# Two block products ahead of the attention, the gate in one piece, and w_v and k squared at other offsets

## The chip, the core and the metric

The kernel runs on one core of a Trainium2 chip. A core has TensorE (PE; its weight loads are listed apart as PEld), VectorE (DVE), ScalarE (ACT), GpSimd (POOL) and DMA queues fed from SyncE (SP). The metric is the device time of one execution in microseconds (us), the median of the runs shown.

## The reference

Local attention in chunks feeds a channel mix of the RWKV kind. Cut to what matters:

```python
# q, k, v: [4, 8, 768, 64]; mem_k, mem_v: [4, 8, 8, 64]; chunks of 32, 16 keys left, 8 right, 8 memory keys
for c in range(nc):
    k_full = concat([mem_k, k[:, :, l_start:r_end]]); v_full = concat([mem_v, v[:, :, l_start:r_end]])
    a = softmax(scale * q_c @ k_full.T)
    out[:, :, c_start:c_end] = a @ v_full
x = out as [4, 768, 512]                       # 3072 tokens
x_prev = x shifted by one token
xk = mu_k * x + (1 - mu_k) * x_prev
xr = mu_r * x + (1 - mu_r) * x_prev
k = relu(xk @ w_k)                             # 512 -> 1024
v = (k * k) @ w_v                              # 1024 -> 512
return sigmoid(xr @ w_r) * v                   # gate: 512 -> 512
```

## The kernel before

The 3072 tokens are worked in 12 units u of 256. Tensors are kept in float32; each operand of a large product is split into a high part in fp32r (names with h: `xh`, `wkh`, `kh`) and the rest (`xl`, `wkl`, `kl`), and a product is three products: high by high, high by low, low by high.

A unit's work on TensorE consists of the hidden product `h` (tile `ph`, four pieces, line 594), the gate `g` (`pr`, two halves, line 570), and the value product `v`. In units 0 to 2 `v` is plain (`pv`, line 570). From unit 3 (`FAST`) on, `seven` makes it as a product of 2x2 blocks by Winograd's scheme: seven block products `v{u}.0` to `v{u}.6` (`part`, line 901, tiles `pa`, `pb`, `pc`, `pd`, twelve instructions of 128x256 each) instead of eight. Their stationary operands are blocks of k squared and sums of them (`a11`, `a12`, `a22`, `s1` to `s4`), made by VectorE in place in the two halves of `k2` (line 865) and split into tile `khl` (`operand`, lines 853 and 857). Their moving operands are quarters of `w_v`, or sums of quarters (`wtbig`, `wtx`) made once by `weight_sums`. `add` and `mul` gather the seven results in the output tiles `o` on VectorE (lines 925 and 936).

Among these stands the attention of later units: `s` (scores of unit u+2, line 406), `t` (transposed probabilities, tile `pt`, line 468), copies of `pt` into block-diagonal tiles `aTz` (`bd`, lines 310 and 312), `a` (tile `px`, line 485), and copies of `px` into `xT`. VectorE and ScalarE also do the softmax (`max`, `sub`, `exp`, `sum`, `norm`), the mix (`df`, `mix`), the splits `xh` and `xl`, and the ReLU, square and sigmoid.

Three things set the order. `te_order` writes out the order of the pieces on TensorE and gives each a due time. A planner (`Plan.order`) then places every operation on its engine by costs and due times, chooses between ACT, DVE and POOL where `either` allows it, and hands out buffers in rings. PSUM has 8 banks of 2 KB per partition: tag `s` two, tag `m` four (`ph`, `pr`, `pv`, and some block products), tag `tp` two (`pt`, `px`, and the others). A bank is taken over when its last reader is done. Each engine then runs its instructions in the planned order.

`split_tiles` and the `const.tile` lines place the weights in SBUF in the order in which they are called; `split_x` and `split_k` cut operands out of tiles at an offset of some elements of 4 bytes.

Of the kernel before, what the change touches and what calls it, by code (L numbers as in the profile page):

```python
# [16 lines left out]
P = 128  # L17
# [192 lines left out]
def te_order():  # L210

    nu = B * S // UTOK
    seq = LEAD.split()
    seq = [tuple([x[0]] + [int(n) for n in x[1:].split(".")]) for x in seq]
    for u in range(1, nu):
        a, b = 2 * u + 2, 2 * u + 3
        g = [("g", u + 1, c) for c in range(QPU) if u + 1 < FAST]
        h = [("h", u, f) for f in range(FT // 2)]
        v = [("v", u, n) for n in range(FT // 2)]
        x = [("a", a), ("a", b)]  # L220
        if u >= FAST:
            g = [("g", u, c) for c in range(QPU)]
            v = [("v", u, n) for n in range(7)]
            seq += h + [("t", a), ("t", b), ("s", u + 2), g[0]] + v[:2] + x + g[1:] + v[2:]
            continue
        seq += h + [("t", a), ("t", b), ("s", u + 2)]
        seq += x + g + v[1:] if u == 1 else v[:1] + x + v[1:] + g
    last = {"s": nu, "g": nu, "t": B * NQT, "a": B * NQT}
    seq = [x for x in seq if x[1] < last.get(x[0], nu)]
    due, t = {}, 8.0  # L230
    for x in seq:
        assert x not in due
        due[x] = t
        t += PART if x[0] == "v" and x[1] >= FAST else PE_COST[x[0]]
    return due
# [3 lines left out]
def local_attention__then__channel_mix(  # L239
# [22 lines left out]
    def sb(tag, shape, name, dt=F32):  # L262
        if isinstance(tag, Slot):
            tag = f"{tag.tag}at{tag.place}"
        return work.tile(shape, dt, tag=tag, name=name, bufs=bufs.get(tag, 1))

    def split_x(tag, name, m):
        if m:
            return sb(tag, [P, KT, UTOK], name, F32R)
        x = sb(tag, [P, 128 + KT * UTOK], name, F32R)  # L270
        return x[:, 48 : 48 + KT * UTOK].rearrange("p (k t) -> p k t", k=KT)

    def split_k(tag, name):
        n = 2 * (int(tag[2:])) + "hl".index(tag[1])
        return khl[:, 16 + n * DM : 16 + (n + 1) * DM]

    def ps(tag, name, n=1):
        return psA.tile([P, n * 512], F32, tag=tag, name=name, bufs=bufs[tag])
# [4 lines left out]
    def split_tiles(n, name):  # L283
        return [
            [const.tile([P, 2 * DM], F32R, tag=f"{name}{s}{i}", name=f"{name}{s}{i}") for i in range(n)]
            for s in "hl"
        ]

    wk_hl, wv_hl, wr_hl = split_tiles(KT, "wk"), split_tiles(FT // 2, "wv"), split_tiles(KT // 2, "wr")
    aTz = [  # L290
        const.tile([P, NPAIR * NJ, 2, CHUNK], F32, tag=f"aTz{i}", name=f"aTz{i}")
        for i in range(bufs["aT"])
# [15 lines left out]
    def copy(e, dst, src):  # L308
        if e is nc.scalar:
            e.copy(dst, src)  # L310
        else:
            e.tensor_copy(dst, src)  # L312
# [248 lines left out]
    def channel_mix(u):  # L561
# [115 lines left out]
        for f in range(FT // 2):  # L677
            def f_relu(e, f=f):
                half = k2[f // 2].rearrange("p i t -> p (i t)")
                r = T["kf", u, f] = half[:, f % 2 * 2 * UTOK : (f % 2 + 1) * 2 * UTOK]  # L680
                if e is nc.scalar:
                    e.activation(r, T["ph", u, f], AF.Relu)  # L682
                else:
                    e.tensor_scalar_max(r, T["ph", u, f], 0.0)  # L684

            def f_sq(e, f=f):
                q = T["kf", u, f]
                if e is nc.scalar:
                    e.activation(q, q, AF.Square)  # L689
                else:  # L690
                    e.tensor_mul(q, q, q)  # L691

            def f_hi(e, f=f):
                h = T["kh", u, f] = split_k(f"kh{f}", f"kh{u}_{f}")
                copy(e, h, T["kf", u, f])

            def f_lo(e, f=f):
                l = T["kl", u, f] = split_k(f"kl{f}", f"kl{u}_{f}")
                e.tensor_sub(l, T["kf", u, f], T["kh", u, f].bitcast(F32))

# [12 lines left out]

# [122 lines left out]
    def seven(u, ks, o_g, sgs):  # L836
# [6 lines left out]
        def operand(name, at, pair, deps):  # L843
            src = A[at]
            kh, kl = Slot(f"kh{pair}"), Slot(f"kl{pair}")
            use = kf[2 * at[1] : 2 * at[1] + 2]

            def view(x):
                return x.rearrange("p (i t) -> p i t", t=P)

            def f_hi(e):
                T["ah", u, name] = view(split_k(kh.tag, f"kh{u}_{name}"))
                copy(e, T["ah", u, name], src)

            def f_lo(e):
                T["al", u, name] = view(split_k(kl.tag, f"kl{u}_{name}"))
                e.tensor_sub(T["al", u, name], src, T["ah", u, name].bitcast(F32))  # L857

            hh = op(f"kh{u}.{name}", either(act=(0.6,), dve=(0.36, True)), f_hi, deps, new=[kh], use=use)
            ll = op(f"kl{u}.{name}", either(dve=(0.62, True), pool=(1.3, True)), f_lo, [hh], new=[kl], use=use + [kh])  # L860
            return hh, ll, kh, kl

        def step(name, out, x, y, deps):
            def f():
                nc.vector.tensor_sub(A[out], A[x], A[y]) if name != "s1" else nc.vector.tensor_add(A[out], A[x], A[y])  # L865

            return op(f"{name}{u}", ("dve", 0.62, True), f, deps, use=kf)

        sq = [x for x, _ in ks]
        a11 = operand("a11", (0, 0), 0, sq[:2])  # L870
        a12 = operand("a12", (0, 1), 1, sq[2:])
        a22 = operand("a22", (1, 1), 2, sq[2:])
        s1 = step("s1", (1, 1), (1, 0), (1, 1), sq[:2] + [a22[1]])
        s3 = step("s3", (1, 0), (0, 0), (1, 0), [s1])
        o1 = operand("s1", (1, 1), 3, [s1])
        s2 = step("s2", (0, 0), (1, 1), (0, 0), [s1, s3, a11[1]])
        s4 = step("s4", (0, 1), (0, 1), (0, 0), [s2, a12[1]])

        def bank(key, tag):
            T[key, u] = ps(tag, f"{key}{u}")  # L880
# [58 lines left out]
                f"{name}u{u}", ("dve", 0.37, True), f, [dep, o_g[at[0]]], use=[os[at[0]], sgs], due=dep.due + 0.6,  # L939
            )  # L940

        def f_keep(e):
            copy(e, spot((0, 1)), T["pa", u][:, :HN])

        os = [Slot("o") for _ in range(QPU)]
        pa, pb, pc, pd = Slot("tp"), Slot("m"), Slot("m"), Slot("tp")
        p1 = part(0, "a11", a11, (0, 0), "pa", 0, pa, [], "tp")
        k1 = op(
            f"keep{u}", either(act=(0.4,), dve=(0.36,)), f_keep, [p1], new=opens(0), use=[pa, os[0]],
            due=p1.due + PART + 0.6,  # L950
        )
        p2 = part(1, "a12", a12, (1, 0), "pa", 1, pa, [])
        c11 = add("c11", (0, 0), (0, 1), "pa", 1, pa, [p2, k1])
        o3 = operand("s3", (1, 0), 0, [s3, p1])
        o2 = operand("s2", (0, 0), 1, [s2, p2])
        p7 = part(2, "s3", o3, 3, "pb", 0, pb, [], "m")
        o4 = operand("s4", (0, 1), 0, [s4, p7])
        p6 = part(3, "s2", o2, 2, "pb", 1, pb, [])
        u2 = add("u2", (1, 0), (0, 1), "pb", 1, pb, [p6, k1])
        p5 = part(4, "s1", o1, 1, "pc", 0, pc, [], "m")  # L960
        u4 = add("u4", (0, 1), (1, 0), "pc", 0, pc, [p5, u2, c11])
        c22 = add("c22", (1, 1), (0, 1), "pb", 0, pb, [u4, p7])
        u3 = add("u3", (1, 0), (1, 0), "pb", 0, pb, [u4, p7])
        p3 = part(5, "s4", o4, (1, 1), "pd", 0, pd, [], "tp")
        c12 = add("c12", (0, 1), (0, 1), "pd", 0, pd, [p3, c22])
        p4 = part(6, "a22", a22, 4, "pc", 1, pc, [])
        c21 = add("c21", (1, 0), (1, 0), "pc", 1, pc, [p4, u3])
        muls = [mul("m11", (0, 0), c11), mul("m22", (1, 1), c22), mul("m12", (0, 1), c12), mul("m21", (1, 0), c21)]
        for c, deps in ((0, [muls[0], muls[2]]), (1, [muls[1], muls[3]])):
            def f_st(c=c):  # L970
# [77 lines left out]
```

## Time and profile before

| | before |
|---|---|
| median of 3 runs | 418.65 us (415.96 to 419.8) |
| the profiled execution, its own time | 418.19 us |
| its span, first to last instruction | 416.3 us |
| mean granted TensorE clock | 0.995 |
| busy: PE, PEld, DVE, ACT, POOL | 399.3, 361.8, 321.8, 207.7, 50.9 us |
| a unit of the second half (units 4 to 9), ph to ph | 31.96 us |

The page gives busy times as shares of the span; the chain of work is followed back from the last instruction; the waits say which engine stood for whom. A row of the time line begins with the start and the duration in us; in the chain likewise. Times between two starts on the same engine tell more of TensorE than durations do, since its products overlap.

### The profile page before, as it was taken

Reading aid. Unit: us, or ns where it says so; the run is one execution under the profiler, and the core shown is the slowest. Engines: PE = TensorE matmul, PEld = TensorE weight load, DVE = VectorE, ACT = ScalarE, POOL = GpSimd, SP = SyncE. Lnnn points to the kernel's source line nnn. Section 1 sums busy time; section 2 is a strip of 40 time slices with the busy share of each in tenths; the row PEclk is TensorE's granted clock in tenths of the full one; section 3 lists DMA queues with packets and bytes.
Section 4 is the critical chain, followed back from the end, with each engine's and each line's share of the span. In section 5 each row is a group of like instructions: output and inputs, shape, how many; then the busy total and the mean of one; then the engine's idle time right before and its main releaser. Section 6 shows DMA issues by size and latency. Waiting matters only on the chain.

```text
span 416.3 us, 10814 instructions
## 1 busy us (share of the span) xinstructions
PE 399.3 (96%) x4787; PEld 361.8 (87%) x4787; DVE 321.8 (77%) x546; ACT 207.7 (50%) x309; POOL 50.9 (12%) x40
## 2 busy tenths in 40 slices
PE   7788999999999999999999999999999999999995
PEld 3446989888988989989989989989989988999995
DVE  3998979997779899489489489479579569669264
ACT  2385792842452763563563554464455455452440
POOL 2202000000000022022022031030130230210000
PEclk9998999999999999999999999999999999999999
DMA  8997955210043070160151152142143103100101
GB/s 328 382 415 249 393 167 177 76 50 27 25 169 138 2 237 18 52 224 31 52 205 52 52 189 66 52 163 93 52 154 101 52 3 102 51 2 2 52 0 50
DMA packets 12910, 48.99 MB, mean 118 GB/s; under 512 B 1472, under 2 KB 1600, under 8 KB 12352
## 3 DMA queue, kind: packets, MB, share of 16 engines
q1 hardware_dynamic: 12864, 48.31, 32.1%
q8 instruction: 37, 0.61, 0.6%
q14 instruction: 9, 0.07, 0.1%
HBM read 42.01 MB, written 6.29 MB: 116 GB/s over the span
## 4 chain that ended last, share of the span: by engine, by line
PE 87%; DVE 6%; DMA 4%; issue 1%; SPq 0%; ACT 0%; DVEq 0%
PE ph L594 32%; PE pr L570 16%; PE pv L570 8%; PE pc L901 6%; PE pb L901 6%; PE pa L901 5%; DMA qk<-in_qk_dram 4%; PE s L406 4%; PE px L485 4%; PE pd L901 3%; PE pt L468 2%; DVE k L865 1%; DVE o L925 1%; DVE khl L312 1%; DVE o L312 1%
## 5 line engine op out<-in xcount | busy, mean ns | idle before, releaser
L594 PE MATMUL ph<-xl,wkh 128*128 128x256 f32 x384 | 106.7, 278 | 0.0
L594 PE MATMUL ph<-xh,wkh 128*128 128x256 f32 x384 | 106.6, 278 | 0.0
L594 PE MATMUL ph<-xh,wkl 128*128 128x256 f32 x384 | 106.4, 277 | 0.0
L594 PEld LDWEIGHTS ph<-xh,wkh 128*128 128x128 f32 x384 | 72.4, 188 | 0.1
L594 PEld LDWEIGHTS ph<-xl,wkh 128*128 128x128 f32 x384 | 72.1, 188 | 0.3 <-DVE xl L553 0.2
L594 PEld LDWEIGHTS ph<-xh,wkl 128*128 128x128 f32 x384 | 72.1, 188 | 0.0
L682 ACT ACTIVATE k<-ph 128x512 f32<-128x512 f32 x45 | 26.9, 597 | 69.2 <-PE ph L594 69.1
L857 DVE TENSOR_TENSOR khl<-k,khl 128x512 fp32r<-128x512 f32 x49 | 32.9, 684 | 22.8 <-ACT khl L310 22.6
L310 ACT CAST khl<-k 128x512 fp32r<-128x512 f32 x54 | 33.4, 618 | 16.6 <-DVE k L865 5.8
L570 PE MATMUL pr<-wrh,xh 128*128 128x512 f32 x96 | 39.6, 412 | 0.0
L570 PE MATMUL pr<-wrl,xh 128*128 128x512 f32 x96 | 37.8, 393 | 0.0
L570 PE MATMUL pr<-wrh,xl 128*128 128x512 f32 (+1 forms) x108 | 37.6, 366 | 0.0
L485 PEld LDWEIGHTS px<-aTz,vw 128*64 128x64 f32 x768 | 25.0, 141 | 10.9 <-DVE o L925 5.4
L312 DVE COPY aTz<-pt 64x512 f32<-64x512 f32 x18 | 11.7, 691 | 29.1 <-ACT aTz L310 29.1
L553 POOL TENSOR_TENSOR xl<-df,xh 128x1024 fp32r<-128x1024 f32 x8 | 19.1, 2391 | 118.1 <-ACT xh L310 118.1
L485 PE MATMUL px<-aTz,vw 128*64 128x64 f32 x768 | 27.9, 229 | 5.6 <-DVE o L925 4.5
L641 ACT ACTIVATE sg<-pr 128x512 f32<-128x512 f32 x24 | 14.3, 599 | 36.5 <-PE pr L570 36.5
L570 PE MATMUL pv<-wvh,khl 128*128 128x512 f32 (+1 forms) x97 | 31.0, 395 | 0.0
L691 POOL TENSOR_TENSOR k<-k 128x512 f32<-128x512 f32 x9 | 9.4, 1039 | 175.3 <-ACT k L682 175.3
L689 ACT ACTIVATE k<-k 128x512 f32<-128x512 f32 x38 | 23.9, 632 | 8.1 <-DVE k L684 7.0
L901 PE MATMUL pa<-wvh,khl 128*128 128x256 f32 x144 | 26.9, 281 | 0.0
L441 DVE TENSOR_TENSOR e<-e,sm_sb 128x1024 f32<-128x1024 f32 x12 | 26.3, 2188 | 0.1
(94 smaller groups left out, 805.5 us busy)
## 6 DMA issues: line engine op xcount, KB each, us to landing
qk<-in_qk_dram SPq DMA_DIRECT2D x24, 768.0 KB, 6.2
vw<-in_vw_dram SPq DMA_DIRECT2D x24, 512.0 KB, 4.2
out_dram<-o SPq DMA_DIRECT2D x24, 256.0 KB, 2.0
raw<-in_w_k_dram SPq DMA_DIRECT2D x4, 1024.0 KB, 8.1
raw<-in_w_v_dram SPq DMA_DIRECT2D x4, 1024.0 KB, 6.7
raw<-in_w_r_dram SPq DMA_DIRECT2D x2, 1024.0 KB, 7.6
id_sb<-in_ident_dram SPq DMA_DIRECT2D x1, 64.0 KB, 6.1
mu_sb<-in_mu_dram SPq DMA_DIRECT2D x1, 4.0 KB, 5.8
```

The lines of the kernel that those rows point to most:

```text
L310: e.copy(dst, src)
L312: e.tensor_copy(dst, src)
L406: nc.tensor.matmul(s5[CHUNK * j : CHUNK * (j + 1), h, c, r, :], q4[z, r, j, :], k4[z, r, j, :], start=True, stop=True,)
L441: g.tensor_mul(e, e, T["sum", u].unsqueeze(2).to_broadcast([P, NG, NK]))
L485: nc.tensor.matmul(p3[64 * h : 64 * h + 64, 2 * g : 2 * g + 2, CHUNK * j : CHUNK * j + CHUNK], v[:, g, h, j, :], a[:, h, g, j, :], start=True,
L553: e.tensor_sub(l, T["xf", u, m], T["xh", u, m].bitcast(F32))
L570: nc.tensor.matmul(p[:, a : a + step], x, w[:, a : a + step], start=start, stop=stop and a + step == DM)
L594: nc.tensor.matmul(z, w, x[:, k], start=start, stop=stop)
L682: e.activation(r, T["ph", u, f], AF.Relu)
L689: e.activation(q, q, AF.Square)
L857: e.tensor_sub(T["al", u, name], src, T["ah", u, name].bitcast(F32))
L901: nc.tensor.matmul(p, l[:, i], r[i], start=i + k == 0, stop=i == FT // 2 - 1 and k == 2)
```

## The change

The order on TensorE from unit 3 on, the scheme's order of steps and of block products, the PSUM tags and the places in SBUF change; the number of instructions on TensorE does not. In the diff, `step`, `operand`, `part`, `add` and `mul` are those shown above.

```diff
@@ te_order
-            seq += h + [("t", a), ("t", b), ("s", u + 2), g[0]] + v[:2] + x + g[1:] + v[2:]
+            seq += h + [("t", a), ("t", b)] + v[:2] + x + [("s", u + 2)] + g + v[2:]
@@ split_x, split_k
-        if m:
-            return sb(tag, [P, KT, UTOK], name, F32R)
-        x = sb(tag, [P, 128 + KT * UTOK], name, F32R)
-        return x[:, 48 : 48 + KT * UTOK].rearrange("p (k t) -> p k t", k=KT)
+        x = sb(tag, [P, 64 * m + KT * UTOK], name, F32R)
+        return x[:, 16 * m : 16 * m + KT * UTOK].rearrange("p (k t) -> p k t", k=KT)
-    def split_k(tag, name):
+    def split_k(tag, off=0):
         n = 2 * (int(tag[2:])) + "hl".index(tag[1])
-        return khl[:, 16 + n * DM : 16 + (n + 1) * DM]
+        return khl[:, off + n * DM : off + (n + 1) * DM]
@@ tiles
-    wk_hl, wv_hl, wr_hl = split_tiles(KT, "wk"), split_tiles(FT // 2, "wv"), split_tiles(KT // 2, "wr")
+    wk_hl, wr_hl = split_tiles(KT, "wk"), split_tiles(KT // 2, "wr")
...
     zero_sb = const.tile([P, P], F32R, tag="zero", name="zero_sb")
+    const.tile([P, 48], F32, tag="gap", name="gap")
+    wv_hl = split_tiles(FT // 2, "wv")
@@ seven
-        a12 = operand("a12", (0, 1), 1, sq[2:])
-        a22 = operand("a22", (1, 1), 2, sq[2:])
-        s1 = step("s1", (1, 1), (1, 0), (1, 1), sq[:2] + [a22[1]])
-        s3 = step("s3", (1, 0), (0, 0), (1, 0), [s1])
-        o1 = operand("s1", (1, 1), 3, [s1])
-        s2 = step("s2", (0, 0), (1, 1), (0, 0), [s1, s3, a11[1]])
-        s4 = step("s4", (0, 1), (0, 1), (0, 0), [s2, a12[1]])
+        s3 = step("s3", (0, 0), (0, 0), (1, 0), sq[:2] + [a11[1]])
+        o3 = operand("s3", (0, 0), 1, [s3])
+        a12 = operand("a12", (0, 1), 2, sq[2:])
+        a22 = operand("a22", (1, 1), 3, sq[2:])
+        s1 = step("s1", (1, 0), (1, 0), (1, 1), [s3] + sq[2:])
+        s2 = step("s2", (1, 1), (1, 1), (0, 0), [s1, a22[1]])
+        s4 = step("s4", (0, 1), (0, 1), (1, 1), [s2, a12[1]])
...
-        pa, pb, pc, pd = Slot("tp"), Slot("m"), Slot("m"), Slot("tp")
-        p1 = part(0, "a11", a11, (0, 0), "pa", 0, pa, [], "tp")
-        p2 = part(1, "a12", a12, (1, 0), "pa", 1, pa, [])
-        c11 = add("c11", (0, 0), (0, 1), "pa", 1, pa, [p2, k1])
-        p7 = part(2, "s3", o3, 3, "pb", 0, pb, [], "m")
-        p6 = part(3, "s2", o2, 2, "pb", 1, pb, [])
-        p5 = part(4, "s1", o1, 1, "pc", 0, pc, [], "m")
-        p3 = part(5, "s4", o4, (1, 1), "pd", 0, pd, [], "tp")
-        p4 = part(6, "a22", a22, 4, "pc", 1, pc, [])
+        pa, pb, pc, pd = Slot("m"), Slot("m"), Slot("tp"), Slot("tp")
+        p1 = part(0, "a11", a11, (0, 0), "pa", 0, pa, [], "m")
+        k1 = keep("ka", (0, 1), 0, p1)
+        p7 = part(1, "s3", o3, 3, "pa", 1, pa, [])
+        k7 = keep("kb", (1, 1), 1, p7)
+        p2 = part(2, "a12", a12, (1, 0), "pb", 0, pb, [], "m")
+        c11 = add("c11", (0, 0), (0, 1), "pb", 0, pb, [p2, k1])
+        p6 = part(3, "s2", o2, 2, "pb", 1, pb, [])
+        p5 = part(4, "s1", o1, 1, "pc", 0, pc, [], "tp")
+        u3 = add2("u3", (1, 0), (1, 0), (1, 1), [u4, k7])
+        p3 = part(5, "s4", o4, (1, 1), "pc", 1, pc, [])
+        p4 = part(6, "a22", a22, 4, "pd", 0, pd, [], "tp")
```

The offset `off` is 48 elements for `pv` (line 694) and 0 for the block products. `keep` copies one side of `pa` into `o`, on ScalarE or VectorE; before, side 0 was copied so and side 1 (the sum c11) was added to it by VectorE from the bank. `add2` is `add` with both inputs in `o`.

Three places show how instructions move. The first is TensorE in unit 7, from the transposes of the probabilities (`pt16`, `pt17`) on; a row is line, operation, output and inputs, shape, and a count. Before:

```order
L468 MATMUL pt16_3336<-id_sb_64,e8_3024 128x128 x4
L468 MATMUL pt17_3342<-id_sb_64,e8_3024 128x128 x4
L406 MATMUL s9_3349<-qk18_3021 32x64 x32
L406 MATMUL s9_3349<-qk19_3027 32x64 x32
L570 MATMUL pr_7_0_3417<-wrh0_82,xh7_1_3213 128x512
```

Now block products (`pa7`) stand there:

```order
L468 MATMUL pt16_3344<-id_sb_64,e8_3135 128x128 x4
L468 MATMUL pt17_3350<-id_sb_64,e8_3135 128x128 x4
L901 MATMUL pa7_3357<-wvh0_86,khl_83 128x256
L901 MATMUL pa7_3357<-wvl0_90,khl_83 128x256
L901 MATMUL pa7_3357<-wvh0_86,khl_83 128x256 x2
```

and behind the 24 products of `pa7`:

```order
L901 MATMUL pa7_3357<-wtx42_1152,khl_83 128x256
L485 MATMUL px16_3392<-aTz0_78,vw16_3020 64x2x32 x16
L485 MATMUL px17_3413<-aTz1_79,vw17_3091 64x2x32 x16
L406 MATMUL s9_3437<-qk18_3108 32x64 x32
L406 MATMUL s9_3437<-qk19_3117 32x64 x32
L570 MATMUL pr_7_0_3509<-wrh0_74,xh7_1_3189 128x512
```

So the scores `s9` and the first gate half moved behind `px`, and both gate halves follow each other; before, `pa7` and the two `px` stood between the halves.

The second place is VectorE in the same unit, around the split of the next unit's `xl8_0` and that of the operand `s4` (an `L857` row that reads `k21`, the second half of k squared). Before, from the step `s4` (`L865`) on:

```order
L865 TENSOR_TENSOR k21_89<-k21_89,k20_88 128x4x128
L533 TENSOR_TENSOR df8_3540<-xT8_3515 128x1024
L435 TENSOR_REDUCE sm_sb_90<-e9_3437 128x16
L436 TENSOR_SCALAR sm_sb_90<-sm_sb_90 128x16
L437 RECIPROCAL sm_sb_90<-sm_sb_90 128x16
L543 SCALAR_TENSOR_TENSOR xf8_3571<-df8_3540,mu_sb_65,xT8_3515 128x256 x4
L857 TENSOR_TENSOR khl_91<-k21_89,khl_91 128x512
L925 TENSOR_TENSOR o7_1_3593<-pb7_3545,o7_0_3472 128x256
L543 SCALAR_TENSOR_TENSOR df8_3540<-df8_3540,mu_sb_65,xT8_3515 128x256 x4
L553 TENSOR_TENSOR xl8_0_3624<-xf8_3571,xh8_0_3591 128x1024
L925 TENSOR_TENSOR o7_0_3472<-pc7_3577,o7_1_3593 128x256
```

and now, from the split of the operand `s2` to that of the operand `s4`, the last row:

```order
L857 TENSOR_TENSOR khl_83<-k21_81,khl_83 128x512
L533 TENSOR_TENSOR df8_3507<-xT8_3430 128x1024
L415 MEMSET s9_3437 32x2x4x16
L419 TENSOR_REDUCE sm_sb_82<-s9_3437 128x16
L543 SCALAR_TENSOR_TENSOR xf8_3526<-df8_3507,mu_sb_65,xT8_3430 128x256 x4
L423 TENSOR_TENSOR e9_3549<-s9_3437,sm_sb_82 128x1024
L543 SCALAR_TENSOR_TENSOR df8_3507<-df8_3507,mu_sb_65,xT8_3430 128x256 x4
L553 TENSOR_TENSOR xl8_0_3572<-xf8_3526,xh8_0_3551 128x1024
L925 TENSOR_TENSOR o7_0_3387<-pb7_3557,o7_0_3387 128x256
L312 CAST khl_83<-k21_81 128x512
L936 TENSOR_TENSOR o7_0_3387<-o7_0_3387,sg7_3547 128x256
L857 TENSOR_TENSOR khl_83<-k21_81,khl_83 128x512
```

The softmax's reduction and subtraction (`L419`, `L423`), both mixes (`L543`) and the split `xl8_0` (`L553`) now stand ahead of the first sum out of `pb7` (`L925`, c11) and the split of `s4`; before, `xl8_0` came behind the latter.

The third place is GpSimd. Before, from the square of units 2 and 3 to the two splits of unit 4:

```order
L691 TENSOR_TENSOR k21_89<-k21_89 128x512 x2
L857 TENSOR_TENSOR khl_91<-k21_89,khl_91 128x512 x2
L553 TENSOR_TENSOR xl4_1_2008<-df4_1906,xh4_1_1975 128x1024
L691 TENSOR_TENSOR k21_89<-k21_89 128x512
L857 TENSOR_TENSOR khl_91<-k21_89,khl_91 128x512 x2
```

and so on in every unit up to 10. Now, from the splits at the program's start to its end:

```order
L365 TENSOR_TENSOR wkl1_71<-mag3_190,wkh1_67 128x1024
L553 TENSOR_TENSOR xl0_0_452<-df0_360,xh0_0_450 128x1024
L691 TENSOR_TENSOR k21_81<-k21_81 128x512 x9
L1055 UNCONDITIONAL_BRANCH
L1055 ISA
```

One square (`L691`) a unit stays on GpSimd; `xl` and two splits into `khl` went to VectorE.

More of the change, by code (lines that the diff above doesn't have):

```diff
@@ L693, in f_hi @@
             def f_hi(e, f=f):
-                h = T["kh", u, f] = split_k(f"kh{f}", f"kh{u}_{f}")
+                h = T["kh", u, f] = split_k(f"kh{f}", 48)
                 copy(e, h, T["kf", u, f])
             def f_lo(e, f=f):
-                l = T["kl", u, f] = split_k(f"kl{f}", f"kl{u}_{f}")
+                l = T["kl", u, f] = split_k(f"kl{f}", 48)
                 e.tensor_sub(l, T["kf", u, f], T["kh", u, f].bitcast(F32))
@@ L851, in f_hi @@
             def f_hi(e):
-                T["ah", u, name] = view(split_k(kh.tag, f"kh{u}_{name}"))
+                T["ah", u, name] = view(split_k(kh.tag))
                 copy(e, T["ah", u, name], src)
             def f_lo(e):
-                T["al", u, name] = view(split_k(kl.tag, f"kl{u}_{name}"))
+                T["al", u, name] = view(split_k(kl.tag))
                 e.tensor_sub(T["al", u, name], src, T["ah", u, name].bitcast(F32))
@@ L940, in mul @@
             )
-        def f_keep(e):
-            copy(e, spot((0, 1)), T["pa", u][:, :HN])
-        os = [Slot("o") for _ in range(QPU)]
-        pa, pb, pc, pd = Slot("tp"), Slot("m"), Slot("m"), Slot("tp")
-        p1 = part(0, "a11", a11, (0, 0), "pa", 0, pa, [], "tp")
[L948 to L951, printed above, removed]
-        p2 = part(1, "a12", a12, (1, 0), "pa", 1, pa, [])
@@ L953, in seven, with keep @@
-        c11 = add("c11", (0, 0), (0, 1), "pa", 1, pa, [p2, k1])
-        o3 = operand("s3", (1, 0), 0, [s3, p1])
-        o2 = operand("s2", (0, 0), 1, [s2, p2])
-        p7 = part(2, "s3", o3, 3, "pb", 0, pb, [], "m")
-        o4 = operand("s4", (0, 1), 0, [s4, p7])
+        def keep(name, at, side, dep):
+            return op(
+                f"{name}{u}", either(act=(0.4,), dve=(0.36,)),
+                lambda e: copy(e, spot(at), T["pa", u][:, side * HN : (side + 1) * HN]), [dep],
+                new=opens(at[0]), use=[pa, os[at[0]]], due=dep.due + PART + 0.6,
+            )
@@ new lines, in add2, with f @@
+        def add2(name, to, x, y, deps):
+            def f():
+                nc.vector.tensor_add(spot(to), spot(x), spot(y))
+            return op(
+                f"{name}u{u}", ("dve", 0.37, True), f, deps, use=[os[at[0]] for at in (to, x, y)],
+                due=deps[0].due + 0.6,
+            )
+        os = [Slot("o") for _ in range(QPU)]
+        pa, pb, pc, pd = Slot("m"), Slot("m"), Slot("tp"), Slot("tp")
+        p1 = part(0, "a11", a11, (0, 0), "pa", 0, pa, [], "m")
+        k1 = keep("ka", (0, 1), 0, p1)
@@ L958, in seven @@
+        p7 = part(1, "s3", o3, 3, "pa", 1, pa, [])
+        k7 = keep("kb", (1, 1), 1, p7)
+        o1 = operand("s1", (1, 0), 0, [s1, p1])
+        o2 = operand("s2", (1, 1), 1, [s2, p7])
+        p2 = part(2, "a12", a12, (1, 0), "pb", 0, pb, [], "m")
+        c11 = add("c11", (0, 0), (0, 1), "pb", 0, pb, [p2, k1])
+        o4 = operand("s4", (0, 1), 2, [s4, p2])
         p6 = part(3, "s2", o2, 2, "pb", 1, pb, [])
         u2 = add("u2", (1, 0), (0, 1), "pb", 1, pb, [p6, k1])
-        p5 = part(4, "s1", o1, 1, "pc", 0, pc, [], "m")
+        p5 = part(4, "s1", o1, 1, "pc", 0, pc, [], "tp")
@@ L961, in seven @@
         u4 = add("u4", (0, 1), (1, 0), "pc", 0, pc, [p5, u2, c11])
-        c22 = add("c22", (1, 1), (0, 1), "pb", 0, pb, [u4, p7])
-        u3 = add("u3", (1, 0), (1, 0), "pb", 0, pb, [u4, p7])
-        p3 = part(5, "s4", o4, (1, 1), "pd", 0, pd, [], "tp")
-        c12 = add("c12", (0, 1), (0, 1), "pd", 0, pd, [p3, c22])
-        p4 = part(6, "a22", a22, 4, "pc", 1, pc, [])
-        c21 = add("c21", (1, 0), (1, 0), "pc", 1, pc, [p4, u3])
+        u3 = add2("u3", (1, 0), (1, 0), (1, 1), [u4, k7])
@@ L968, in seven @@
+        c22 = add2("c22", (1, 1), (0, 1), (1, 1), [u4, u3])
+        p3 = part(5, "s4", o4, (1, 1), "pc", 1, pc, [])
+        c12 = add("c12", (0, 1), (0, 1), "pc", 1, pc, [p3, c22])
+        p4 = part(6, "a22", a22, 4, "pd", 0, pd, [], "tp")
+        c21 = add("c21", (1, 0), (1, 0), "pd", 0, pd, [p4, u3])
         muls = [mul("m11", (0, 0), c11), mul("m22", (1, 1), c22), mul("m12", (0, 1), c12), mul("m21", (1, 0), c21)]
```

## The prediction

> **What bounds the kernel now.** I read the page's shares first, then the chain that ended last, then who waits on TensorE, then the time line of one unit.
>
> ```profile
> PE 399.3 (96%) x4787; PEld 361.8 (87%) x4787; DVE 321.8 (77%) x546; ACT 207.7 (50%) x309; POOL 50.9 (12%) x40
> PE 87%; DVE 6%; DMA 4%; issue 1%; SPq 0%; ACT 0%; DVEq 0%
> PE px L485 <- DVE o L925: 4.5, 7, 0.7
> PEld px L485 <- DVE o L925: 5.4, 7, 0.8
> ```
>
> TensorE is busy 96% of the span and holds 87% of the chain, so time can come off only where it waits or where its products run slower than they could. The waits (total, times, longest) name one place: the attention products px wait seven times for a VectorE sum, 5.4 us seen from the weight loads. For the second loss I lay the chain (start, us, what) of unit 7 beside a few other units:
>
> ```profile
> 104.88 11.31 PE ph L594 x96
> 163.29 11.05 PE ph L594 x96
> 259.31 10.90 PE ph L594 x96
> 275.48 2.84 PE pa L901 x24
> 281.25 2.95 PE pr L570 x13
> 284.20 2.83 PE pb L901 x24
> 287.02 1.41 PE pc L901 x12
> 383.62 1.59 PE pc L901 x12
> 385.21 11.31 PE ph L594 x96
> 402.11 2.75 PE pr L570 x13
> ```
>
> and the busy time of each engine in three stretches (columns: us; busy PE, PEld, DVE, ACT, POOL; granted clock; DMA share, GB/s):
>
> ```profile
> 104.00:116.00 12.00, 12.00 (x101) 11.89 (x100) 8.85 (x22) 6.27 (x11) 0.00 (x0) 1.00 0.06 22
> 259.15:291.10 31.95, 31.25 (x407) 29.66 (x406) 23.82 (x42) 16.33 (x24) 5.97 (x5) 1.00 0.29 100
> 385.00:396.00 11.00, 11.00 (x95) 11.00 (x95) 2.67 (x7) 4.31 (x7) 0.00 (x0) 1.00 0.13 49
> ```
>
> A product of 128x256 takes 10.90/96 = 113.5 ns in ph of unit 7, but 1.41/12 = 117.5 to 2.84/24 = 118.3 ns in every block product of the same shape, and 11.31/96 = 117.8 ns in ph of units 2 and 11. The granted clock is 1.00 in all three stretches, so this is a second pace of the same instruction. A gate half takes 2.95 us behind px and 2.75 us in the last unit, where no px stands ahead of it.
>
> **The change, part by part.**
>
> *The wait for c11 goes.*
>
> ```profile
> 151.13 2.14 PE L485 MATMUL px<-aTz,vw 128*64 128x64 f32 x64
> 278.24 1.15 PE L485 MATMUL px<-aTz,vw 128*64 128x64 f32 x32
> 280.09 1.15 PE L485 MATMUL px<-aTz,vw 128*64 128x64 f32 x32 [0.70 <-DVE o L925]
> 281.18 0.50 PE L570 MATMUL pr<-wrh,xh 128*128 128x512 f32 x1
> 279.62 0.42 DVE L925 TENSOR_TENSOR o<-pa,o 128x256 f32<-128x256 f32 x1
> ```
>
> The second px takes over the bank of pa (tag tp) and starts when c11 has drained it (279.62 + 0.42 = 280.04). Both px last 281.18 - 278.24 = 2.94 us here and about 2.1 us in unit 3, where nothing holds them. After the change pa and pb have tag m; px takes over the banks of pt alone. What is late next is the copies of pt into aTz, which had 278.24 - 271.01 = 7.2 us of TensorE work as cover and now have pa's 2.84:
>
> ```profile
> 270.05 1.04 PE L468 MATMUL pt<-id_sb,e 128*128 128x128 f32 x8
> 271.01 1.48 PE L406 MATMUL s<-qk 64*32 64x64 f32 x128
> 271.34 1.30 DVE L312 COPY aTz<-pt 64x512 f32<-64x512 f32 x2 [3.90 <-ACT aTz L310]
> 270.74 1.05 ACT L310 COPY aTz<-pt 64x512 f32<-64x512 f32 x2
> ```
>
> They end at 271.34 + 1.30 = 272.64; px could start at 271.01 + 2.84 = 273.85. They stay hidden by 1.2 us. The operands a11 and s3, which pa now needs right behind pt, come from the squares of ph 0 and 1 alone, while ph 2 and 3 (5.4 us) still run. On the DMA queue the two vw loads now stand ahead of the two qk loads; each is for the next unit, some 30 us away. **Term: -5.4 us.**
>
> *The gate in one piece.* Its second half no longer stands behind px: 2.95 - 2.75 = 0.2 us in each of units 3 to 10. The first half still follows an attention product (s), and px to s or pt to pa has no row of before; the nearest joint costs that same 0.2, so each is worth between -0.2 and +0.2, and I take 0, since one disappears (pt to s) and one is new (pt to pa). **Term: 8 x 0.2 = -1.6 us.**
>
> *Small stalls.* ph of unit 4 waited for its xl (11.05 against 10.90) and one pc in unit 10 (1.59 against 1.41). Both operands now come earlier on their engine. **Term: -0.3 us.**
>
> *Other offsets.* From the built programs, in bytes within a partition: the moving operand of a block product (w_v, and the sums wt) begins 64 past a multiple of 128 before and on a multiple after; its stationary operand (khl) the other way round. The new pair is that of ph (x on a multiple, w_k 64 past it), modulo 256 too. ph is the nearest row, so I take its pace for the 9 x 7 x 12 = 756 products: 756 x (117.8 - 113.5) ns. The bounds are that and 0 (the pace of ph in units 2 and 11, with the same offsets). **Term: -3.25 us.**
>
> [...]
>
> The first three units' value products (pv) get an offset pair that no product has here. The gate's 2.75/12 = 229 ns and twice 117.8 = 236 ns bound the 145 of them within 1 us; I take 0. The same for s, px and pt, whose tiles also move: 4.4 us a unit by 4% would be 0.2 us a unit either way, unseen, 0 taken.
>
> *VectorE takes over GpSimd's work* (one xl and two kl a unit).
>
> ```profile
> 132.72 1.22 DVE L441 TENSOR_TENSOR e<-e,sm_sb 128x1024 f32<-128x1024 f32 x1
> 291.64 2.55 DVE L441 TENSOR_TENSOR e<-e,sm_sb 128x1024 f32<-128x1024 f32 x1
> 290.72 2.39 POOL L553 TENSOR_TENSOR xl<-df,xh 128x1024 fp32r<-128x1024 f32 x1 [14.93 <-ACT xh L310]
> 275.79 0.68 DVE L865 TENSOR_TENSOR k<-k,k 128x512 f32<-128x512 f32 x1
> 276.50 0.69 DVE L865 TENSOR_TENSOR k<-k 128x512 f32<-128x512 f32 x1
> 282.10 0.68 DVE L865 TENSOR_TENSOR k<-k,k 128x512 f32<-128x512 f32 x1
> 282.70 1.22 DVE L533 TENSOR_TENSOR df<-xT 128x1024 f32<-128x1024 f32 x1
> 283.83 1.21 DVE L435 TENSOR_REDUCE sm_sb<-e 128x16 f32<-128x1024 f32 x1
> 285.46 1.58 DVE L543 SCALAR_TENSOR_TENSOR xf<-df,mu_sb,xT 128x256 f32<-128x256 f32 x4
> 286.95 0.69 DVE L857 TENSOR_TENSOR khl<-k,khl 128x512 fp32r<-128x512 f32 x1
> 287.56 0.42 DVE L925 TENSOR_TENSOR o<-pb,o 128x256 f32<-128x256 f32 x1
> 287.89 1.67 DVE L543 SCALAR_TENSOR_TENSOR df<-df,mu_sb,xT 128x256 f32<-128x256 f32 x4
> 289.47 1.22 DVE L553 TENSOR_TENSOR xl<-xf,xh 128x1024 fp32r<-128x1024 f32 x1
> 381.96 1.21 DVE L553 TENSOR_TENSOR xl<-xf,xh 128x1024 fp32r<-128x1024 f32 x1
> ```
>
> The unit's VectorE (23.82 us of 31.95 in the stretch shown above) gains 1.22 + 2 x 0.69 = 2.6 us and loses 1.3, since the norm took 2.55 us beside GpSimd's xl and 1.22 alone: about 25 of 30.6 us. That fits on average. What counts is the run from the aTz copies to kl of s4, which the fourth of the five last block products (pc, side 1) needs. From the rows: the copies 1.3; seven operations of 128x512 at 282.70 - 282.10 = 0.6, 4.2; two casts, c11 and a multiplication at 287.89 - 287.56 = 0.33, 1.3; df, sub and xl at 283.83 - 282.70 = 1.13, 3.4; max like the reduction 1.2; the two mix 1.5 and 1.6 (to the next start); kl itself 0.7: 15.3 us with the roundings. The run starts 271.34 - 270.05 = 1.3 us behind pt, so kl ends 16.6 us behind it. TensorE gets there after pt 0.96, pa 2.84, px 2.1, s 1.4, gate 2.95 + 2.75, three parts 4.24: 17.2 us, or 16.95 at the faster pace. Cover of 0.4 to 0.6 us: **no term**, and a rival.
>
> **Sum:** 5.4 + 1.6 + 0.3 + 3.25 = 10.55 us. The profiled execution took 418.19 us (span 416.3), hence 407.6; against the median 418.65, 0.46 higher, the same sum gives 408.1.
>
> **The rivals.**
>
> *The pace doesn't follow the offsets.* For: ph itself has both paces at one place. Against: no block product ran at 113.5 but a few. 418.19 - 7.3 = 410.9. The same time comes out if the parts gain 3.25 and ph loses it. [...]
>
> *ph falls to the slow pace.* ph is fast where its xl ended just ahead of it (unit 8: 289.47 + 1.22 = 290.69, ph at 291.26) and slow in unit 11, whose xl ended at 383.17, two microseconds ahead. The change puts xl 5 us ahead of ph in every unit. Price: 8 x (11.31 - 10.90) = 3.3 us; with parts unchanged 414.2.
>
> *VectorE sets the pace, mildly.* Half a microsecond a unit beyond the cover: 8 x 0.5 = 4 us, 411.6 to 414.9.
>
> *VectorE sets the pace so far that the kernel is slower.* An operation that needs the one before it follows after 0.71 us (275.79 to 276.50) instead of 0.6 (282.10 to 282.70). Were each of the run's some 20 operations held by 0.1, by its predecessor or by ACT's casts, kl of s4 would be 2.0 us later, TensorE would stand 1.45 us at pc in 8 units, and 11.6 us would outweigh the sum: 419.2. It decides from a delay of 0.55 + 10.55/8 = 1.9 us a unit. Against: the order interleaves dependent operations.
>
> *The change doesn't free px*, because another copy takes c11's place: 418.
>
> **How the numbers follow.** The forecast 407.6 has 0.40; 410.9 (by either way) 0.27; 414.2 0.15; mild VectorE 0.10; slower 0.05; nothing freed 0.03. The point is 407.6. The range runs from 404.5 (forecast, less 0.8 for ph of units 2 and 11 and up to 2 for pv, s, px and pt) to 414.5, leaving out about 0.13. No change can be told from one within 1% (4.2 us). Faster by more holds the first two, half of the third and most of the mild case: 0.83; within 1%: 0.11; slower 0.06.
>
> **What would show it.** In the profile after: no row of px waiting for o; both px in about 2.1 us; the two gate halves in some 5.7 us together; block products at 1.36 us for twelve instead of 1.41; ph still 10.90; VectorE near 25 us a unit, POOL with one operation a unit. Wrong would be: a wait of pc for khl, ph at 11.31, or block products at 1.41.

## The result and the profile after

| kernel | median, us | kernel before beside it, us | ratio of the two, 95% interval |
|---|---|---|---|
| after the change | 416.41 (412.27 to 420.02) | 418.64 | 0.9933 (0.9915 to 0.9952) |

The ratios here and below are taken from fast executions alone, without two of these 20 and two of the 12 of experiment 6 that ran slow; the medians include them. The change saves 0.7%, some 2.8 us by the ratio, where 10.55 us were forecast; 416.4 lies above the range. The profiled execution took 417.12 us, with a span of 415.3 us. Its shares, its chain by engine, and from the list of waits (total, times, longest) three rows:

```profile
PE 395.8 (95%) x4787; PEld 360.0 (87%) x4787; DVE 328.4 (79%) x566; ACT 207.2 (50%) x319; POOL 16.4 (4%) x19
...
PE 89%; DVE 5%; DMA 3%; issue 2%; SPq 0%; DVEq 0%
```

```profile
PE s L406 <- issue: 5.5, 4, 2.5
PEld pc L901 <- DVE khl L857: 3.9, 9, 0.9
PE pc L901 <- DVE khl L857: 2.1, 8, 0.7
```

GpSimd's work is gone, as forecast, and so is every wait of px for o. Two other rows took its place: block product pc waits for khl, and the scores s wait for nothing that the profile can name ("issue"). The chain through unit 7 (start, us, what) shows both:

```profile
272.14 2.02 PE px L485 x64
274.16 1.38 PE s L406 x87
275.54 1.56 issue
277.10 0.30 PE s L406 x3
277.40 5.67 PE pr L570 x25
283.07 2.75 PE pb L901 x24
285.82 0.02 issue
285.85 0.42 DVE o L925
286.27 0.33 DVE khl L312
286.61 0.33 DVE o L936
286.94 0.61 DVE khl L857
287.55 0.04 issue
287.60 1.42 PE pc L901 x10
289.02 1.36 PE pd L901 x12
```

Both px take 2.02 us instead of 2.94, the gate is one piece of 5.67, and pd takes 1.36 where twelve products took 1.41: three steps of the forecast, to be read off. But s stands still for 1.56 us three products before its end, and from pb to pc the chain leaves TensorE for VectorE: c11 (`o L925`), cast of s4, m11, split of s4, and only then the rest of pc.

Stage by stage, in us from the first product of a stage to the first of the next, from the profiled executions ("unit" is a unit of the second half without a stop of s):

```
          ph    pt    pa    px    s     pr    pb    pc    pd    unit
before  10.90  0.97  2.92  2.94  1.41  5.75  2.83  2.83  1.41  31.96
after   10.89  0.79  3.00  2.01  1.41  5.62  2.74  3.21  1.36  31.03
```

In after, s took 1.91, 3.24 and 2.83 us in units 3, 7 and 8, together 3.75 us of stops. pc of units 3 to 9 stopped for 0.49 us each, that of unit 10 for 0.95 and of unit 11 for 0.35: 4.7 us.

### The profile page after: what moved, and what is told of

The parts are those of the page before. It is cut to its first block, busy times and chain, and to the rows that moved or that the text cites. A ratio compares the mean times of both kernels' runs of the same rounds, so it can differ in the third digit from the quotient of the medians.

```text
span 415.3 us, 10804 instructions
## 1 busy us (share of the span) xinstructions
PE 395.8 (95%) x4787; PEld 360.0 (87%) x4787; DVE 328.4 (79%) x566; ACT 207.2 (50%) x319; POOL 16.4 (4%) x19
## 4 chain that ended last, share of the span: by engine, by line
PE 89%; DVE 5%; DMA 3%; issue 2%; SPq 0%; DVEq 0%
PE ph L594 32%; PE pr L570 16%; PE pv L570 8%; PE px L485 6%; PE pa L901 6%; PE pb L901 6%; PE s L406 4%; DMA qk<-in_qk_dram 3%; PE pc L901 3%; PE pt L468 3%; PE pd L901 3%; PE warm L1008 2%; DVE khl L857 1%; DVE o L925 1%; DVE o L936 1%
## 5 line engine op out<-in xcount | busy, mean ns | idle before, releaser
L857 DVE TENSOR_TENSOR khl<-k,khl 128x512 fp32r<-128x512 f32 x63 | 42.6, 687 | 29.1 <-ACT khl L310 28.8
L570 PE MATMUL pr<-wrh,xh 128*128 128x512 f32 x96 | 38.6, 402 | 0.0
L310 ACT CAST khl<-k 128x512 fp32r<-128x512 f32 x51 | 31.7, 623 | 8.9 <-PE pv L570 2.5
L641 ACT ACTIVATE sg<-pr 128x512 f32<-128x512 f32 x24 | 14.3, 598 | 33.1 <-PE pr L570 33.1
L406 PE MATMUL s<-qk 64*32 64x64 f32 x1536 | 19.1, 230 | 9.9 <-issue 5.5
L406 PEld LDWEIGHTS s<-qk 64*32 64x32 f32 x1536 | 16.5, 107 | 13.8 <-issue 9.7
L485 PE MATMUL px<-aTz,vw 128*64 128x64 f32 x768 | 26.3, 228 | 1.2 <-issue 1.2
L570 PEld LDWEIGHTS pr<-wrh,xl 128*128 128x128 f32 x108 | 20.3, 188 | 4.4
L691 POOL TENSOR_TENSOR k<-k 128x512 f32<-128x512 f32 x9 | 9.4, 1042 | 320.5 <-ACT k L682 320.5
```

The lines of the kernel that those rows point to most:

```text
L406: nc.tensor.matmul(s5[CHUNK * j : CHUNK * (j + 1), h, c, r, :], q4[z, r, j, :], k4[z, r, j, :], start=True, stop=True,)
L485: nc.tensor.matmul(p3[64 * h : 64 * h + 64, 2 * g : 2 * g + 2, CHUNK * j : CHUNK * j + CHUNK], v[:, g, h, j, :], a[:, h, g, j, :], start=True,
L570: nc.tensor.matmul(p[:, a : a + step], x, w[:, a : a + step], start=start, stop=stop and a + step == DM)
L641: nc.scalar.activation(T["sg", u][:, c * DM : (c + 1) * DM], T["pr", u, c], AF.Sigmoid)
```

## The experiments

All times and ratios are against runs of the kernel before on the same chip.

| experiment | median, us | before, us | ratio, 95% interval |
|---|---|---|---|
| 1 c11 behind s4 | 410.15 | 417.78 | 0.981 (0.9779 to 0.9841) |
| 2 and s early | 409.88 | 417.78 | 0.981 (0.978 to 0.984) |
| 3 as 1, loads late | 411.24 | 417.78 | 0.9834 (0.9808 to 0.986) |
| 4 offsets alone | 414.69 | 417.78 | 0.9912 (0.9878 to 0.9945) |
| 5 as 1, s behind the gate | 409.0 | 418.84 | 0.9762 (0.9726 to 0.9798) |
| 6 order alone | 420.24 | 418.84 | 1.003 (0.9999 to 1.0061) |
| 7 order, c11 behind s4 | 414.67 | 418.84 | 0.991 (0.9877 to 0.9943) |
| 8 as 1, instructions shifted | 412.25 | 418.84 | 0.9855 (0.9821 to 0.9889) |
| 9 as 1, pa right behind ph | 410.94 | 418.31 | 0.9818 (0.9773 to 0.9862) |
| 10 as 9, px behind the gate | 411.99 | 418.31 | 0.9842 (0.9802 to 0.9883) |

### What holds pc

In after, VectorE stands idle ahead of c11 in unit 5 (time line, start, us):

```profile
220.09 1.22 DVE L553 TENSOR_TENSOR xl<-xf,xh 128x1024 fp32r<-128x1024 f32 x1
220.43 1.52 PE L901 MATMUL pb<-wtbig,khl 128*128 128x256 f32 x12
...
221.99 0.42 DVE L925 TENSOR_TENSOR o<-pb,o 128x256 f32<-128x256 f32 x1 [0.69 <-PE pb L901]
222.34 0.42 DVE L312 CAST khl<-k 128x512 fp32r<-128x512 f32 x1
...
223.00 0.69 DVE L857 TENSOR_TENSOR khl<-k,khl 128x512 fp32r<-128x512 f32 x1
223.75 0.51 PE L901 MATMUL pc<-wvh,khl 128*128 128x256 f32 x2 [0.20 <-DVE khl L857]
```

c11 adds the first side of pb, which was complete about when the second side began (220.43); yet it started only when the second side was done too. The cast of s4 overwrites the operand that the first side read, so it was free to go by then as well, but it stood behind c11 in VectorE's queue. Experiment 1 puts c11 behind the split; the multiplication m11 (line 936), which needs c11, goes with it:

```diff
-        c11 = add("c11", (0, 0), (0, 1), "pb", 0, pb, [p2, k1])
         o4 = operand("s4", (0, 1), 2, [s4, p2])
+        c11 = add("c11", (0, 0), (0, 1), "pb", 0, pb, [p2, k1, o4[1]])
```

> The changed kernel with one edit: the sum c11 stands behind the two splits of the operand s4 on VectorE; nothing else moves on any engine but u2 and c11. Theory 'c11 blocks the queue': in the changed kernel VectorE stood 0.69 us before c11 (221.99), although c11 needs only the first side of pb, since it started only after the second side was done, and the cast and split of s4 stood behind it. Then the stop of pc goes: 0.48 us in seven units, 0.95 in unit 10 and 0.34 in unit 11, 4.7 us in all; pc from 3.21 to about 2.72 us; 416.4 becomes about 411.7. Rival 'VectorE is too full': its run of operations up to the split of s4 is simply longer than TensorE's way there, as the rival of the prediction had it; then the split comes when it came, pc keeps 3.1 to 3.2 us, and the time stays within 1 us of 416.4.

Its time line at the same place:

```profile
219.03 1.23 DVE L553 TENSOR_TENSOR xl<-xf,xh 128x1024 fp32r<-128x1024 f32 x1
220.16 0.43 DVE L312 CAST khl<-k 128x512 fp32r<-128x512 f32 x1
220.69 0.69 DVE L857 TENSOR_TENSOR khl<-k,khl 128x512 fp32r<-128x512 f32 x1
221.30 0.75 DVE L925 TENSOR_TENSOR o<-pb,o 128x256 f32<-128x256 f32 x2
...
222.29 0.39 PE L901 MATMUL pc<-wvh,khl 128*128 128x256 f32 x2
```

The cast follows xl at once, the split ends at 221.38, and pc needs it at 222.29: 0.9 us to spare. pc takes 2.72 us in all nine units. The time falls by 1.2 points of the ratio, 5 us (4.7 expected). So VectorE was not too full; c11 held its queue. The edit takes the work of c11 and m11 (0.33 us each) off the way to the split along with c11's wait, so it doesn't tell the two apart; the time line of after does, since only the wait of 0.69 us was missing from the forecast's run (see below).

The trace of before shows the same kind of wait in every unit from 3 on. In unit 7 the first side of `pa` was done at 276.9; VectorE, idle, still began its copy of that side (`keep`) only behind the last product of the second side, 1.15 us later than it could have:

```profile
278.03 0.28 PE L901 MATMUL pa<-wvh,khl 128*128 128x256 f32 x1
278.35 0.42 DVE L312 COPY o<-pa 128x256 f32<-128x256 f32 x1 [1.15 <-PE pa L901]
```

### Why s stops

In the records of after, the stops of s in units 3, 7 and 8, and one of 2.5 us in s2 at the start, each come where TensorE's instruction count (products, weight loads and waits) passes some 193 more than a multiple of 256. (The start has one more stop named "issue", 1.20 us of px at 26.80; it stands at 140 of 256 and is of another kind.) The trace also has the transfers of 16,384 bytes on the queue of instructions, 37 on the page:

```profile
q8 instruction: 37, 0.61, 0.6%
```

```
stop in     instruction   ahead of it 128   last transfer    stop ends
            mod 256       products took     ended            after it
s2          194           4.9 us            33.51 us         1.48 us
s unit 3    194           2.40              149.51           1.30
s unit 7    194           1.66              275.78           1.32
s unit 8    193           2.1               308.01           1.36
```

The 4787 products with as many weight loads make 37.4 stretches of 256, against 37 transfers. If each piece of 16,384 bytes serves one such stretch, an estimate from these two counts, that is 64 bytes to an instruction, and 128 products with their weight loads to a piece. The trace of before had such a stop too, in its start, which I had not read:

```profile
30.43 1.35 PE L406 MATMUL s<-qk 64*32 64x64 f32 x112 [0.48 <-DMA qk<-in_qk_dram]
33.78 0.47 PE L406 MATMUL s<-qk 64*32 64x64 f32 x16 [2.00 <-issue]
```

Experiment 2 keeps the edit of 1 and puts s back behind pt, apart from px:

```diff
-            seq += h + [("t", a), ("t", b)] + v[:2] + x + [("s", u + 2)] + g + v[2:]
+            seq += h + [("t", a), ("t", b), ("s", u + 2)] + v[:2] + x + g + v[2:]
```

> The kernel of the run before, with the scores s back between pt and the block products, as before the change; the gate stays in one piece. In the changed kernel s of units 3, 7 and 8 stopped for 0.24, 1.56 and 1.22 us with nothing that they waited for, each time within 1.4 us of the end of a 16 KB instruction transfer. Theory 'instructions run dry': px and s back to back are 192 products with 192 weight loads in 3.5 us, more than a transfer brings; apart, with 24 slow block products between, there is no stop: s 1.41 us in every unit from 3 on, and the time 1 to 3.5 us below the run before; two joints cost up to 0.2 us a unit. Rival 'the stops come and go by chance, with other transfers': s stops in some units here too, and the time is that of the run before or up to 1.6 us above it.

s takes 1.41 us in every unit from 3 on; no stop of TensorE over 60 ns is left behind the start. But the time equals that of experiment 1. Its units 4 to 9 take 30.85 to 31.21 us, against 30.43 to 30.52 there in units without a stop: s behind pt costs 0.17, pc still waits for 0.13 to 0.19 us, and ph is at its slow pace in units 5 and 7 (11.31). The stops went; the new order gave the gain back.

Experiment 3 keeps px and s together and issues the loads of vw and qk elsewhere:

```diff
+    made = {o.name: o for o in plan.ops}
+    for u in range(FAST, NU):
+        for name in [f"vw{2 * u + 4 + c}" for c in range(2)] + [f"qk{2 * u + 6 + c}" for c in range(2)]:
+            if name in made:
+                made[name].deps.append(made[f"out{u}.1"])
```

> The first kernel of this list (c11 behind s4) with px and s back to back, but the loads of vw and qk for the next units are issued behind the output of the unit, some 20 us after s, and not at px and s. Theory 'instructions run dry': px and s are as dense as they were, so s stops in some units as before, by 0.2 to 1.6 us, and the time is that of the first kernel within 1 us. Rival 'the loads delay the instruction transfer': the transfer at 274.18 took 1.60 us instead of 0.95 and stood right behind the vw loads issued at 273.27; without loads there it takes 0.95 us, s stops nowhere by more than 0.3 us, and the time is 1 to 3 us below the first kernel.

s stops at the same three products, by 0.5, 1.54 and 1.05 us. From 271 to 273.7 us, around the stop of unit 7, its DMA queues carried the instructions alone, and no load:

```profile
q8 instruction: 1, 0.02, 3.1%
```

The time is 411.24 us. The rival falls: loads may lengthen a transfer (1.60 and 1.68 us in unit 7 of after and of experiment 1, 1.32 here), but don't make the stop.

Experiment 8 moves the boundaries. 32 small products on zeros at the start (64 records), in place of one warm-up product (2 records), shift every later instruction by 124:

```diff
-                for _ in range(n):
+                for _ in range(n - (o.name == "s1")):
...
+                if o.name == "s1":
+                    for _ in range(32):
+                        nc.tensor.matmul(warm[:, :64], zero, zero[:, :64], start=True, stop=True)
```

> The first experiment's kernel (c11 behind s4) with 32 small products on zeros (128x64, 64 records of TensorE) put ahead of the scores s1 at the start in place of one warm-up product: 62 records, 124 instructions more; nothing else changes. Theory 'instructions run dry at each 16 KB': the boundaries move back by 62 products, from product 87, 63, 41, 16, 125, 103, 79 of s in units 3 to 9 to 25, 1, 107, 82, 63, 41, 17. So s of unit 5 stops, by 0.5 to 1.3 us, that of unit 6 by 0 to 0.4 us, and those of units 3, 7 and 8, which stopped until now, run through; the stop of 2 us in s2 at the start goes too. Time 1 to 4 us below the first experiment. Rival 'the stops belong to these units' data or loads': s stops in units 3, 7 and 8 as before, and the time is the same or later by the small products (up to 2 us).

The stops moved as expected: units 3, 7 and 8 run through, s2 too, and s stops in units 5 (0.91 us in all) and 6 (0.52). From its time line:

```profile
183.44 0.39 PE L570 MATMUL pr<-wrh,xl 128*128 128x512 f32 x1 [0.62 <-issue]
...
211.96 1.32 PE L406 MATMUL s<-qk 64*32 64x64 f32 x108
213.94 0.41 PE L406 MATMUL s<-qk 64*32 64x64 f32 x20 [0.66 <-issue]
```

What I had left out are boundaries just behind s: the gate of unit 4 stops at its third product (first row; 0.78 us in all), and that of unit 0 for 1.67 us at 55.21 (1.82 in all), both again at about 193 of 256. The four stops take 1.82 + 0.78 + 0.91 + 0.52 = 4.0 us, as long as the three of experiment 1 (1.05 + 1.99 + 0.90), and the time is no better (412.25), against my 1 to 4 us. The place of the stops is shown to follow the instruction count; shifting them buys nothing.

Experiment 5 sets 25 slow products between px and s:

```diff
-            seq += h + [("t", a), ("t", b)] + v[:2] + x + [("s", u + 2)] + g + v[2:]
+            seq += h + [("t", a), ("t", b)] + v[:2] + x + g + [("s", u + 2)] + v[2:]
```

> The first experiment's kernel (c11 behind s4), with the scores s moved from behind px to behind both gate halves. Theory 'instructions run dry': the stops stand at every 256th instruction of TensorE, 16 KB, where the 128 products ahead of it took under about 2.4 us (2.40, 1.66 and under 3 us with part of px and s in them). With 25 gate products of 227 ns ahead of s, the last 128 products take that little only where the boundary falls on the last five of s; so s stops in one unit at most. Against that stand joints: px to gate 0.1 to 0.2 us, s to pb up to 0.3 us a unit. Time 408 to 410.5 us. Rival 'the stops hang on s alone, however it stands': s stops in two or three units again, and with the joints the time is 410.5 to 413 us.

The chain through its unit 7 runs without "issue":

```profile
270.89 2.02 PE px L485 x64
272.91 5.69 PE pr L570 x25
278.60 1.42 PE s L406 x89
280.02 2.94 PE pb L901 x24
282.96 2.72 PE pc L901 x24
```

s stops nowhere from unit 3 on, and the joints cost 0.21 us a unit (30.73 against 30.52). At 409.0 us, ratio 0.9762, it is the fastest of the kernels here by its median, and clearly ahead of before and after. Its interval overlaps that of experiment 1, so the gain over it of 0.5 points, 2 us, is not shown by the times alone. The profiled executions agree with it: units 3 to 9 take 215.8 us here and 217.9 there, 2.1 us less, although the joints cost 7 x 0.21 = 1.5 us. So the stops cost about 3.6 us, near the 3.9 that experiment 1 shows.

Counted over the twelve profiled executions, TensorE stopped at 29 of the 433 boundaries between stretches of 256 instructions. What tells them apart is the transfer of the piece: all 29 stops ended 1.1 to 1.55 us after the end of that transfer, and at the other 404 it had ended 1.6 us or more ahead. From unit 0 on, the stops stood behind 128 products of 1.66 to 2.45 us. That bound isn't sharp, since boundaries behind some 2.5 us (unit 9 of after) and 1.90 us (unit 5 of experiment 2) passed without a stop. It doesn't hold for s2, which stopped behind 4.9 us in after and 5.45 in before; there the transfer itself set out late, at 32.45 us in after and 31.27 in before, 4.9 us behind the boundary ahead in both (0.3 to 1.05 us in units 3, 7 and 8 of after), and why stays open.

### What the offsets and the order are worth alone

Experiment 4 is the kernel before with the new places in SBUF alone (`split_x`, `split_k`, the `gap` tile and the place of `wv_hl` as in the diff of the change).

> The kernel before with the new offsets alone (w_v, k squared, xh and xl), the order of all engines as before. Theory 'the offsets set the pace of the block products': 113.5 instead of 118 ns in 60 to 84 of a unit's products in nine units, 2.3 to 3.3 us, and about 0.8 us from the value products of units 0 to 2, at 227 instead of 233 ns: 418.6 becomes 414.5 to 415.5. Rival 'what stands ahead sets the pace, not the offsets': block products stay at 117.5 to 118 ns, and the time is within 0.5 us of 418.6.

It took 414.69 us. In its chain pb, pc and pd of a unit run at the fast pace (2.74, 1.36 and 1.36 us), pa does not (2.84), and px waits for c11 as before:

```profile
249.99 2.74 PE pb L901 x24
...
272.93 2.84 PE pa L901 x24
...
277.15 0.35 DVE o L925
277.54 1.15 PE px L485 x32
```

A unit takes 31.67 us instead of 31.96, and the value products of units 1 and 2 take 33.1 instead of 33.9. So offsets do act on the pace: pb took 2.74 us here and 2.83 in before.

Experiment 6 is the changed kernel with the offsets of before, experiment 7 the same with c11 behind s4 (the edit of 1).

> The changed kernel with the offsets of before: its new order alone. The offsets alone gave 414.7 against 417.8 us, 3.1 us. If the parts of the change add up, the order alone gives 416.4 + 3.1 = 419.5 us, no gain or a slight loss, with block products at 117.5 to 118 ns, both px at 2.01 us, pc with its stop. Rival 'the new order alone makes the block products fast': 416 to 417 us, pb and pc at 113.5 ns.

> The kernel of the run before with c11 behind the splits of s4. If the parts add up, 410.2 + 3.1 = 413.3 us: the new order is worth 4 to 5 us once c11 doesn't hold the split of s4. Rival: without the faster pace TensorE gets to pc later, the split is in time by itself and c11's place is worth less than 2 us here, so 416 us or above.

The order alone gains nothing (1.003); with c11 moved it gains 0.9%. The parts add up: 0.9912 x 1.003 = 0.994 for both (0.9933 measured), and c11's place is worth 1.2 points with either set of offsets. So the whole gain of the change as it stands came from the offsets; what the order saved at px, pc and s took away. In 7 the gate behind the stop of 1.78 us in unit 7 took 7.21 us instead of 5.58, while the granted clock was down (column behind the counts in the row below, 0.83). That the stop brought the clock down is not shown; behind a stop of 1.72 us in unit 7 of experiment 1 the gate took 5.59.

```profile
278.00:286.00 8.00, 8.00 (x42) 6.91 (x41) 6.30 (x12) 3.69 (x5) 0.00 (x0) 0.83 0.39 156
```

### Why pa stays slow

> The first experiment's kernel (c11 behind s4) with the order ph, pa, pt, s, first gate half, px, second gate half, then the other block products. In every kernel so far pa took 2.91 to 3.02 us behind pt or behind the gate half after s, and 2.72 in unit 11, where it stands right behind ph. Theory 'what stands ahead slows pa': pa takes 2.72 to 2.76 us in units 3 to 10 too, if its operands are ready, 0.28 us less; s behind pt and the split gate cost back 0.2 to 0.4 us a unit; s stops nowhere; 408 to 411 us. Rival 'pa is slow by its own operands and only the last unit differs': pa keeps 2.9 to 3.0 us, and the time is 410 to 413 us. If a11 or s3 come too late for a place right behind ph, a wait of pa for khl shows it, and the time says nothing on the pace.

> As the run before, but with both px behind both gate halves: ph, pa, pt, s, gate, px, other block products. Theory: pa as fast as there; the gate in one piece saves 0.1 to 0.2 us a unit, and pb behind px costs 0.1; but the mix of the next unit starts 2.8 us later on VectorE, and ph has 6.8 us of block products as its cover instead of 9.6. If that is too short, ph waits for xl by 0.5 to 2 us in every unit, 412 to 424 us; if it is long enough, 407 to 410 us.

The edits are `seq += h + v[:2] + [t, t, s, g[0]] + x + g[1:] + v[2:]` and `seq += h + v[:2] + [t, t, s] + g + x + v[2:]`, with the edit of 1. In 9:

```profile
222.55 1.36 PE pd L901 x12
223.91 10.88 PE ph L594 x96
234.79 2.73 PE pa L901 x24
...
253.45 1.41 PE pd L901 x12
254.87 11.31 PE ph L594 x96
266.17 2.83 PE pa L901 x24
```

pa right behind ph takes 2.73 us in five of eight units, so it isn't slow by its operands alone: its pace went with what stood ahead. In the other three (2.83) ph ahead of it was slow too (11.31 and 11.46), and in units 7 and 8 pd ahead of that (1.41). Neither order is measured faster than experiment 5: in 9 the gate is in two pieces again (5.81) and pc waits for 0.24 to 0.27 us in most units; in 10, as its expectation said it might, ph waits for xl in units 4 to 10, up to 1 us, and is slow in several of them (11.46 us in units 5, 7 and 10).

## Why the prediction was wrong

Term by term, from the two profiled executions:

```
term                         forecast   measured
px waits for c11              -5.4       -6.1   6 x 0.92 + 0.48 + 0.06
gate in one piece             -1.6       -1.0   8 x 0.13
joints px-s, pt-pa             0         -0.5   pt less 0.17, pa more 0.08 a unit
small stalls                  -0.3       -0.3   ph of units 3, 4 and 11
pace of block products        -3.25      -2.4   pb, pc, pd, and pa of unit 11 only
pace of pv                     0         -0.8
pc waits for the split of s4   0         +4.7
s stops                        0         +3.75
first ph later                 0         +1.3   39.27 to 40.56
sum                          -10.55      -1.35  (times: 418.19 to 417.12, -1.07)
```

- **Right:** the wait of px goes; the gate saves, though 0.13 a unit and not 0.2; the offsets make block products faster by 4.3 ns. There the bound of pv (within 1 us, 0 taken) held and its sign was a gain.
- **The step that failed first** is "Cover of 0.4 to 0.6 us: **no term**". The length of VectorE's run was right: the split of s4 was to end 16.6 us behind pt, and in experiment 1, where c11 and m11 (0.66 us) stand behind it, it ends at 221.38, 16.2 behind (pt began at 205.16). What failed is that I counted c11 as 0.33 us of work and gave it no wait. In unit 5 of after the split ended at 223.69, 17.48 behind pt (206.21); without c11's wait of 0.69 (from 221.30 to 221.99) that is 16.8, near the forecast 16.6 and ahead of TensorE, which reached the product that needs it some 17.2 behind pt. c11 read the first side of a bank whose second side TensorE was still writing, and in before c11 read the second side, the last to be written. The copy of `pa`'s first side in before, shown above, had this wait of 1.15 us, and I didn't carry it over to c11. The order quoted ahead of the prediction showed c11 ahead of the cast of s4, and nowhere did I ask what c11 waits for. The rival "VectorE sets the pace, mildly" named the place and nearly the price (0.5 us a unit), but as a run that is too long and not as a wait of c11, and had 0.10.
- **The second** is "px to s ... I take 0": I priced the joint, not what standing together does to the instructions: 192 products with their loads in 3.5 us. Two rows were there to warn of it, the stop of s2 in before, and the page's row of instruction transfers.
- **The third** is the count of 756 in the pace: pa's 24 products a unit kept 118 ns everywhere but in unit 11. Size 0.9 us, made good by pv.
- The later first ph can't be put to the change: among the twelve profiled executions it stands anywhere from 36.6 to 40.7 us.

## What to carry to other kernels

When an operation moves ahead of others in a queue, write down what it waits for and not only how long it lasts; in this kernel a read of one side of a PSUM bank waited for the products of the other side too (0.69 us for c11, 1.15 for the copy in before; whether the chip asks for that wait or the program alone, no run here tells). Count instructions as well as time: in this kernel TensorE stood still, for 0.24 to 1.56 us in s of after, behind stretches of 256 instructions that small products had issued in 1.66 to 2.40 us, at places that can be counted. And a change that removes one wait is judged by experiments on its parts: here the part that was to bring most brought nothing until one addition was moved.

## What was not expected of the hardware

In these profiles the pace of the 128x256 products of ph went with that of pd ahead of it. With the new offsets ph and block products share it: in experiments 2 and 9 a slow pd (1.41) is followed by a slow ph (11.31), a fast one (1.36) by a fast ph (10.89). With the old offsets it is reversed: in experiment 6 ph takes 11.31 behind a pd of 1.36, and 10.90 behind one of 1.41:

```profile
254.97 1.36 PE pd L901 x12
256.33 11.31 PE ph L594 x96
...
288.06 1.41 PE pd L901 x12
289.48 10.90 PE ph L594 x96
```

That fits the two paces (10.90 and 11.31 us) that ph alone showed in the prediction's rows. What sets the pace stays open. In experiment 9 pd took 1.41 us in units 6 and 7, behind a pc of 2.99 with its wait, and 1.36 in units 4, 5, 8 and 9, behind one of 2.96 or 2.97; that the wait decides it is not shown. And pa behind pt is slow with either set of offsets in nearly every unit: 2.83 us in units 3 to 10 of after, and in all of these but unit 8 (2.74) of experiment 6.
